# Another order of all operations, and each input tile laid out as its own block in memory, in an induced-attention and mixture-of-experts kernel

## Chip, cores and metric

One core of a Trainium2 chip, all arithmetic in fp32. The metric is the device time of one execution in microseconds (us). Before the change the median of three executions is 218.88 us (218.73 to 219.15).

## What is computed

Four batches of 11,456 points of 128 numbers pass through two attentions. In the first, 32 learned points attend to all points of a batch; in the second, every point attends to the 32 results. A mixture of eight experts with four slots each follows: softmax over all 45,824 points gives each slot its input, the experts work on 32 slot rows, and softmax over the 32 slots mixes their outputs back to every point.

```python
def mab(q, kv):
    s = scale * (q @ kv.transpose(0, 2, 1))
    s = s - s.max(-1, keepdims=True)
    a = np.exp(s)
    a /= a.sum(-1, keepdims=True) + 1e-09
    return a @ kv
h = mab(I, x)            # I: 32 learned points
x = mab(x, h)            # 45,824 rows of 128
logits = x @ phi         # 32 slots
d = softmax(logits, over all rows);  slot_input = d.T @ x
slot_out[e] = relu(slot_input[e] @ w1[e]) @ w2[e]     # e = 0..7
c = softmax(logits, over the 32 slots)
out = c @ slot_out
```

## The kernel before

The points are cut into 24 tiles, six to a batch (tiles 0 to 5 are batch 0, 6 to 11 batch 1, and so on), each of 15 blocks of 128 rows, 128 x 1920 numbers or 960 KB. A tile comes in twice, by rows (`xn`) and transposed (`xt`); for tiles 0 to 5 the transposed form is made on TensorE (`tp`, L294) and not loaded. All loads and stores are issued on SyncE's queue (SP), in the order of the program: loads of `xn` at L272, of `xt` at L282, of the expert weights `w` at L727, stores of the output at L989. Most large tiles share 13 buffers (the ring 'x'), for `xn`, `xt`, `w` and the output alike, so a load can start only when an earlier tile's last reader is done; `xt` of tiles 9 and 15, and of 10 and 16, each share a region inside the large tile `l_all`.

What each tile passes through, with the names used below (the number behind a name is the tile, or the batch for `u`, `ha`, `hp`, `hs`, `htp`, `hts`, `hb`, `gp`):

- **First attention.** `s1p` = scores on TensorE (L317), maximum on VectorE (`s1`, L328), maximum over a group of three tiles (`pm`, L356), exponential on ScalarE (L374), transpose on VectorE (`e1`, L377), sum over the points on TensorE (`ha`, L393). A batch ends with `hp`, `hs`, `htp` and `hts` (L441 to L455), which give the 32 results transposed, and `hb` (L467).
- **Second attention.** `s2p` = scores (L317, same helper), transpose on VectorE (`bt`, L563), maximum (`bm`, L566), subtraction on GpSimd (L570), exponential on ScalarE, transposes on TensorE (`tt`, L579), logits on TensorE (`lp`, L592), reciprocal of the sum (`bz`, L604), logits into `l_all` (L611), the scaled weights on GpSimd (L622).
- **Softmax over points.** Per segment of three tiles: `pt`, `mc`, `pb` give a running maximum; `d` on GpSimd or VectorE (L693), exponential, and `u` on TensorE (L706), which sums weighted rows per slot.
- **Softmax over slots.** Maximum `cm` (L498), `ct` = subtraction on GpSimd (L504, L507), exponential, sum `cz` (L528, or half sums `ch` on GpSimd at L519 for the tiles in the list CHALF), reciprocal (L534), product on GpSimd (L942), transpose on VectorE into `l_all` (L945).
- **Experts.** After the last `u`, slot inputs (`sit`), first layer `hpm` (L849), transposed hidden rows `htm` (L862), copied to `ma` and `mb` (L867), second layer `so` (L878). Beside it GpSimd forms `vs` and `vr` (L807 to L814), which `zpp` (L833) sums into the denominators `rz_l`; `sos`, `sr` and `srs` (L885 to L891) give the scaled result.
- **Output.** `po` on TensorE (L970) after `srs`, four PSUM tiles for one tile of points, evicted to `ot` by ScalarE or VectorE (L981; the lists OD and OD2 say which of the four VectorE takes), and stored in one to four pieces.

Nothing of the order is decided at run time or by a scheduler: about 1,090 operations are registered by name with their readers and writers, and the string ORDER, two base-62 digits to an operation, is the order in which their instructions are written. Each engine runs its own in that order.

Of the kernel before, what the change touches and what calls it, by code (L numbers as in the profile page):

```python
# [1099 lines left out]
```

## Time and profile before

| | |
|---|---|
| median of three executions | 218.88 us |
| the profiled execution | 219.14 us, its span 217.4 us |
| TensorE, VectorE, ScalarE, GpSimd busy | 86%, 75%, 63%, 58% |
| HBM read, written | 49.84 MB, 23.59 MB |
| first output matmul starts | 154.70 us |
| mean granted clock of TensorE | 0.919 |

Times in rows are microseconds from the start of the span. A row of a timeline gives start, duration and the instruction; in brackets stands the idle time of the engine before it and what ended it ("issue": nothing that the profile shows). PE is TensorE, PEld its weight loads, DVE VectorE, ACT ScalarE, POOL GpSimd. The 1.74 us by which the execution's own time exceeds the span lie around it.

### The profile page before, as it was taken

The numbers are of one execution on the slowest core, as the hardware profiler recorded it, in microseconds if no ns is written. First come the engines' busy times: TensorE is split into PE (matmuls) and PEld (weight loads), VectorE is DVE, ScalarE is ACT, GpSimd is POOL, SyncE is SP. The second block draws the span as 40 slices with busy tenths as digits, with TensorE's granted clock in tenths as the row PEclk, the third lists the DMA queues.
The fourth block names the chain that finished last, engine by engine and source line by source line (L and its number), as shares of the span: only waits on it lengthen the run. The fifth ranks groups of instructions, "written<-read, shape, count | busy, mean of one in ns | idle before, by whom it ended". The sixth has DMA issues, their size and how long they took to land.

```text
span 217.4 us, 6883 instructions
## 1 busy us (share of the span) xinstructions
PE 186.5 (86%) x2788; PEld 126.3 (58%) x2788; DVE 162.8 (75%) x374; ACT 136.0 (63%) x369; POOL 125.2 (58%) x138
## 2 busy tenths in 40 slices
PE   7699989999997999999999899998899988736400
PEld 7459565598543897539886399797546433212100
DVE  0114585999997999999998899967889878875400
ACT  3569441984653995358966688633599977963410
POOL 0000000557899798585998689999866855643000
PEclk9999999999999999999999999999996967975555
DMA  7999999998799999999999960000099999999994
GB/s 221 389 428 420 413 421 414 370 404 358 214 362 425 414 416 414 414 380 413 414 417 413 420 270 3 6 5 3 19 385 415 407 424 411 423 409 425 411 419 202
DMA packets 12414, 73.87 MB, mean 340 GB/s; under 512 B 1632, under 2 KB 2272, under 8 KB 12384
## 3 DMA queue, kind: packets, MB, share of 16 engines
q1 hardware_dynamic: 11952, 73.27, 83.6%
q8 instruction: 22, 0.36, 0.7%
q10 hardware_dynamic: 432, 0.17, 0.3%
q14 instruction: 8, 0.07, 0.1%
HBM read 49.84 MB, written 23.59 MB: 338 GB/s over the span
## 4 chain that ended last, share of the span: by engine, by line
PE 35%; DMA 28%; ACT 12%; DVE 9%; POOL 5%; issue 4%; SPq 1%; ACTq 0%; DVEq 0%; POOLq 0%
DMA xt<-xt 13%; ACT ot L981 8%; DMA out<-ot 8%; PE ha L393 7%; PE s2p L317 6%; PE lp L592 5%; DMA xn<-xn 4%; PE s1p L317 3%; PE tp L294 3%; DMA l_all<-xt 3%; PE tt L579 3%; PE so L878 2%; PE u L706 2%; POOL d L693 2%; PE po L970 1%
## 5 line engine op out<-in xcount | busy, mean ns | idle before, releaser
L970 PE MATMUL po<-l_all,srs 32*128 32x480 f32 x192 | 40.4, 780 | 9.7 <-DVE l_all L945 6.7
L981 ACT COPY ot<-po 128x480 f32<-128x480 f32 x65 | 33.0, 592 | 10.5 <-PE po L970 7.6
L970 PEld LDWEIGHTS po<-l_all,srs 32*128 32x128 f32 x192 | 17.6, 233 | 31.1 <-ACT ot L981 9.3
L570 POOL TENSOR_TENSOR bt<-bt,bm 128x480 f32<-128x480 f32 x24 | 23.6, 997 | 14.9 <-DVE bm L566 14.8
L942 POOL TENSOR_TENSOR ct<-ct,cz 128x480 f32<-128x480 f32 x24 | 23.8, 997 | 13.2 <-DVE cz L534 12.9
L592 PE MATMUL lp<-bdg,a2t 128*128 128x132 f32 x192 | 25.0, 277 | 0.4 <-issue 0.4
L328 DVE TENSOR_SCALAR_CACHE_REDUCE s<-s1p 128x480 f32<-128x480 f32 (+1 forms) x24 | 15.1, 643 | 13.5 <-PE s1p L317 13.0
L622 POOL TENSOR_TENSOR bt<-bt,bz 128x480 f32<-128x480 f32 x24 | 23.6, 1002 | 2.5 <-DVE bz L604 1.3
L507 POOL TENSOR_TENSOR ct<-l_all,cm 128x512 f32<-128x512 f32 x20 | 21.0, 1054 | 5.8 <-DVE l_all L945 4.0
L693 POOL TENSOR_TENSOR d<-l_all,m_all 128x512 f32<-128x512 f32 x19 | 21.8, 1169 | 4.0 <-ACT m_all L672 4.0
L592 PEld LDWEIGHTS lp<-bdg,a2t 128*128 128x128 f32 x192 | 23.1, 190 | 1.2 <-issue 1.1
L317 PE MATMUL s1p<-xt,it_sb 128*32 128x480 f32 x160 | 19.7, 571 | 2.9 <-DVE bm L566 1.6
L981 DVE COPY ot<-po 128x480 f32<-128x480 f32 x31 | 18.8, 635 | 3.7 <-PE po L970 3.7
L317 PE MATMUL s2p<-xt,hts 128*32 128x480 f32 x160 | 20.1, 570 | 0.6 <-issue 0.6
L374 ACT ACTIVATE s<-s,negm 128x480 f32<-128x480 f32 (+1 forms) x24 | 16.7, 701 | 4.9 <-DVE negm L359 4.9
L393 PE MATMUL ha<-xn,e 128*32 128x128 f32 x570 | 19.3, 274 | 0.0
L945 DVE STREAM_TRANSPOSE l_all<-ct 128x480 f32<-128x480 f32 x24 | 15.8, 662 | 4.4 <-POOL ct L942 4.1
L330 POOL MEMSET s<- 128x16 f32 x4 | 0.4, 111 | 31.0 <-DVE e L377 30.7
L511 ACT ACTIVATE ct<-ct 128x480 f32<-128x480 f32 x24 | 14.7, 621 | 5.7 <-POOL ct L507 5.6
L696 ACT ACTIVATE d<-d 128x512 f32<-128x512 f32 x24 | 14.9, 628 | 5.4 <-POOL d L693 4.2
L393 PEld LDWEIGHTS ha<-xn,e 128*32 128x32 f32 x570 | 16.5, 110 | 2.4 <-issue 0.9
L377 DVE STREAM_TRANSPOSE e<-s 128x480 f32<-128x480 f32 x24 | 15.5, 653 | 2.8 <-ACT s L374 2.4
(133 smaller groups left out, 372.1 us busy)
## 6 DMA issues: line engine op xcount, KB each, us to landing
out<-ot SPq DMA_DIRECT2D x20, 960.0 KB, 8.1
xn<-xn SPq DMA_DIRECT2D x18, 960.0 KB, 12.1
xt<-xt SPq DMA_DIRECT2D x14, 960.0 KB, 14.0
w<-w SPq DMA_DIRECT2D x8, 960.0 KB, 10.8
l_all<-xn SPq DMA_DIRECT2D x5, 960.0 KB, 9.5
l_all<-xt SPq DMA_DIRECT2D x4, 960.0 KB, 7.3
out<-ot SPq DMA_DIRECT2D x6, 480.0 KB, 4.9
out<-ot SPq DMA_DIRECT2D x4, 240.0 KB, 2.4
```

What stands on the lines that cost most here:

```text
L317: nc.tensor.matmul(dst[32 * g : 32 * g + 32, :w], lhs, src, start=True, stop=True)
L374: nc.scalar.activation(t[:, :v], t[:, :v], AF.Exp, bias=T["negm", b, g], accum_out=z6[:, a : a + 1])
L393: nc.tensor.matmul(ha[32 * q : 32 * q + 32, :P], T["e1", a][:, j * S : (j + 1) * S], T["xn", a][:, j * P : (j + 1) * P], start=c == lo and ...
L507: nc.gpsimd.tensor_tensor(t.rearrange("p (a e s) -> p a e s", s=S, e=2), l_blocks(n), m, op=ALU.subtract)
L570: nc.gpsimd.tensor_tensor(t, t, T["bm", n][:, :nb].unsqueeze(2).broadcast_to(full), op=ALU.subtract)
L592: nc.tensor.matmul(pt[:, q * 4 * SZ : (q * 4 + m) * SZ], t[: m * S, q * P : (q + 1) * P], bdgs[b % 2].rearrange("p q s -> p (q s)")[: m * ...
L622: nc.gpsimd.tensor_tensor(t, t, T["bz", n][:, :nb].unsqueeze(2).broadcast_to(full), op=ALU.mult)
L693: e.tensor_tensor(t.rearrange(o, s=S, e=2), l_pairs(n), m, op=ALU.subtract)
L942: nc.gpsimd.tensor_tensor(t, t, T["cz", n][:, :nb].unsqueeze(2).broadcast_to([P, nb, S]), op=ALU.mult)
L945: nc.vector.transpose(l_of(n), T[ck][:, :w])
L970: nc.tensor.matmul(ptile("mm", ("po", 4 * n + g))[:, :w], T["srs",][q, :], l_of(n)[q, :], start=True, stop=True)
L981: (nc.vector.tensor_copy if dve else nc.scalar.copy)(ot[:, g * w : (g + 1) * w], T["po", m][:, :w])
```

## The change

Three edits go together. First, a new ORDER string. Second, four lists: GpSimd's half sums are made for tile 22 and no longer for tile 10, and VectorE evicts 30 of the output's 96 pieces where it took 31. Third, the tensors in HBM: before, `xn` holds a batch as 128 long rows (46,080 bytes each) and `w` as 128 rows of 65,536 bytes, from which a tile's 7,680 bytes per row are cut; now each tile of `xn`, `xt` and `w` is one contiguous block of its own (H is 1, so `parts` changes nothing on the chip's side). The sizes of the transfers, the order of the loads and the layout of the output are as before.

```diff
@@ -34,36 +35,41 @@
...
-CHALF = [9, 10, 11, 12, 14, 16]
+CHALF = [9, 11, 12, 14, 16, 22]
...
-OD = [0, 1, 2, 7, 11, 15, 17, 18, 22, 23]
-OD2 = [0, 2, 3, 4, 5, 7, 8, 9, 10, 11, 12, 13, 14, 16, 17, 18, 19, 20, 21, 22, 23]
+OD = [0, 1, 2, 7, 11, 12, 15, 17, 18, 22, 23]
+OD2 = [0, 2, 3, 4, 7, 8, 9, 10, 11, 12, 13, 14, 16, 17, 18, 19, 21, 22, 23]
...
+H = 1
...
 ORDER = (
-    "000102030e0p0A0L0W3z3D0406080507090a0b0c0f0h0j0l0g0i0k0m0q0u0s0n0w0r0t0v0x0B0H0y0C0D0E0F0G0M0Q0d0o0z1718191a0O0S0N0I1f0
...
+    "000102030e0p0A0L0W0406080507090a0b0c0f0h0j0l0g0i0k0m0q0s0u0w0n0r0t0v0x0B0y0D0H0F0d0o0z17180M190C0E0G0I0N1a1f1i1g1j0Q0O0
...
 )
...
+SHAPES = {
+    "x0": (P, XW), "xn": (NT - 1, H, P, XW // H), "xt": (len(HOST_T), H, C, XW // H), "ind_t": (C, S), "phi": (C, S),
+    "w12": (NW, H, P, XW // H), "w3": (P, 2 * E * F - NW * WP), "consts": (P, 2 * P + 5),
+}
...
@@ -180,6 +186,9 @@
         o = l_end(tag) - XW
         T[kind, a] = l_all[:, o : o + XW]
         return T[kind, a]
+
+    def parts(t):
+        return t.rearrange("p (h w) -> p h w", h=H)
 
     def blocks(t):
         return t.rearrange("p (j s) -> p j s", s=S)
@@ -268,8 +277,10 @@
         def ldn(lo, hi):
             def f():
                 t = T["xn", a] if ("xn", a) in T else xtile("xn", a)
-                o = STARTS[c] * P
-                nc.sync.dma_start(t[:, lo:hi], xn[b, :, o + lo : o + hi])
+                if a:
+                    nc.sync.dma_start(parts(t), xn[a - 1].rearrange("h p w -> p h w"))
+                else:
+                    nc.sync.dma_start(t[:, lo:hi], x0[:, lo:hi])
 
             return f
 
@@ -279,7 +290,7 @@
         if a in HOST_T:
 
             def ldt():
-                nc.sync.dma_start(xtile("xt", a)[:, :xw], xt_d[HOST_T.index(a)][:, :xw])
+                nc.sync.dma_start(parts(xtile("xt", a)), xt_d[HOST_T.index(a)].rearrange("h p w -> p h w"))
 
             op("DMA", 2.50 * nb / 16, ("ldt", a), ldt, (), [("xt", a)], [(tag_of("xt", a), ("xt", a))])
             return
@@ -724,7 +735,10 @@
 
             def ld(o=o, m=m):
                 t = btile("x", ("w", o // WP))
-                nc.sync.dma_start(t[:, :m], w12[:, o : o + m])
+                if m == WP:
+                    nc.sync.dma_start(parts(t), w12[o // WP].rearrange("h p w -> p h w"))
+                else:
+                    nc.sync.dma_start(t[:, :m], w3)
                 wt.append(t)
 
             op("DMA", 2.50 * m / 2048, ("ldw", o // WP), ld, (), [("w", o // WP)], [("x", ("w", o // WP))])
@@ -1047,7 +1061,7 @@
...
-    xn = np.zeros((B, P, J * C), np.float32)
+    xn = np.zeros((NT, P, XW), np.float32)
...
@@ -1057,22 +1071,28 @@
...
-        xn[b, :, j0 * C : (j0 + nb) * C] = t.reshape(P, nb * C)
+        xn[a] = t.reshape(P, nb * C)
...
+    def cut(t):
+        return np.ascontiguousarray(t.reshape(-1, P, H, XW // H).transpose(0, 2, 1, 3))
+
...
+    w12 = np.concatenate([w1.reshape(C, E * F), w2.reshape(P, E * F)], axis=1)
...
-        "xn": xn,
-        "xt": xt,
+        "x0": xn[0],
+        "xn": cut(xn[1:]),
+        "xt": cut(xt),
...
-        "w12": np.concatenate([w1.reshape(C, E * F), w2.reshape(P, E * F)], axis=1),
+        "w12": cut(w12[:, : NW * WP].reshape(P, NW, WP).transpose(1, 0, 2)),
+        "w3": np.ascontiguousarray(w12[:, NW * WP :]),
...
```

Line numbers of the changed kernel are 9 to 14 higher. In the rows that follow, a name is followed by the tile (or batch) and then by a running number of the buffer.

**TensorE, end of batch 0's first attention.** Before:

```order
L317 MATMUL s1p_9_410<-l_all_78,it_sb_76 32x480 x4
L393 MATMUL ha_0_1_420<-l_all_78,e1_3_380 32x128 x15
L393 MATMUL ha_0_1_420<-l_all_78,e1_4_415 32x128 x15
L441 MATMUL hp_0_459<-zt_0_418,cst_70 128x1
L393 MATMUL ha_0_1_420<-l_all_78,e1_5_438 32x128 x15
L317 MATMUL s1p_10_476<-l_all_78,it_sb_76 32x480 x4
L317 MATMUL s1p_11_481<-xt_11_332,it_sb_76 32x480 x4
L452 MATMUL htp_0_501<-cst_70,hs_0_499 128x128
L467 MATMUL hb_0_505<-hs_0_499,cst_70 128x128
L317 MATMUL s2p_0_507<-xt_0_118,hts_0_503 32x480 x4
```

Now:

```order
L328 MATMUL s1p_8_394<-xt_8_334,it_sb_76 32x480 x4
L404 MATMUL ha_0_1_412<-l_all_78,e1_3_403 32x128 x15
L404 MATMUL ha_0_1_412<-l_all_78,e1_4_405 32x128 x15
L452 MATMUL hp_0_448<-zt_0_446,cst_70 128x1
L404 MATMUL ha_0_1_412<-l_all_78,e1_5_450 32x128 x15
L328 MATMUL s1p_9_467<-l_all_78,it_sb_76 32x480 x4
L328 MATMUL s1p_10_472<-l_all_78,it_sb_76 32x480 x4
L463 MATMUL htp_0_487<-cst_70,hs_0_485 128x128
L328 MATMUL s1p_11_493<-xt_11_338,it_sb_76 32x480 x4
L328 MATMUL s2p_0_509<-xt_0_114,hts_0_489 32x480 x4
```

The scores of tile 9 (`s1p_9`) stood in front of the sums `ha` of tiles 3 to 5 and stand behind them; `s1p_11` stood in front of `htp_0` and stands behind it; `hb_0` stood in front of the first `s2p` and stands further down.

**TensorE, scores of batch 2 among work of batches 0 and 1.** Before:

```order
L317 MATMUL s1p_14_1007<-xt_14_923,it_sb_76 32x480 x4
L317 MATMUL s1p_17_1016<-xt_17_927,it_sb_76 32x480 x4
L317 MATMUL s1p_15_1021<-l_all_78,it_sb_76 32x480 x4
L579 MATMUL tt_6_1038<-cst_70,bt_6_883 128x128 x3
L579 MATMUL tt_6_1038<-cst_70,bt_6_883 96x128
L579 MATMUL tt_7_1043<-cst_70,bt_7_889 128x128 x3
L579 MATMUL tt_7_1043<-cst_70,bt_7_889 96x128
L662 MATMUL pt_1_1048<-cst_70,tm_1_887 32x128 x3
L706 MATMUL u_0_950<-d_2_1030,bt_2_554 32x32 x15
L317 MATMUL s1p_16_1069<-l_all_78,it_sb_76 32x480 x4
```

Now:

```order
L328 MATMUL s1p_14_1005<-xt_14_898,it_sb_76 32x480 x4
L328 MATMUL s1p_16_1010<-l_all_78,it_sb_76 32x480 x4
L717 MATMUL u_0_970<-d_2_934,bt_2_604 32x32 x15
L328 MATMUL s1p_15_1039<-l_all_78,it_sb_76 32x480 x4
L673 MATMUL pt_1_1044<-cst_70,tm_1_845 32x128 x3
L590 MATMUL tt_6_1065<-cst_70,bt_6_847 128x128 x3
L590 MATMUL tt_6_1065<-cst_70,bt_6_847 96x128
L328 MATMUL s1p_17_1074<-xt_17_902,it_sb_76 32x480 x4
```

`s1p_17`, the sixth `xt` tile of its batch to be loaded, was the fourth of the six scores and is the last; `s1p_16`, `u` and `pt_1` moved ahead of it. In the same way `s1p_23` stood ahead of `s1p_22` and stands behind it. Some rows earlier, `s2p_10` was third of its group, behind `s2p_6` and `pt_0`; it is second now, ahead of both.

**GpSimd, experts.** Before:

```order
L748 MEMSET ma_2410 128x1440
L942 TENSOR_TENSOR ct_6_1408<-ct_6_1408,cz_6_1890 128x480
L507 TENSOR_TENSOR ct_8_2552<-l_all_78,cm_8_1647 128x512
L507 TENSOR_TENSOR ct_9_2554<-l_all_78,cm_9_1680 128x512
L942 TENSOR_TENSOR ct_7_1900<-ct_7_1900,cz_7_2157 128x480
L811 TENSOR_TENSOR vs_2559<-vs_2559,wl_2405 128x32
L519 TENSOR_TENSOR ch_9_2645<-ct_9_2554 128x240
L807 TENSOR_TENSOR vs_2559<-vs_2559,us_all_82 128x32
L814 TENSOR_TENSOR vr_2648<-vs_2559,us_all_82 128x128
L507 TENSOR_TENSOR ct_10_2652<-l_all_78,cm_10_1857 128x512
```

Now:

```order
L762 MEMSET ma_2468 128x1440
L825 TENSOR_TENSOR vs_2470<-vs_2470,wl_2405 128x32
L821 TENSOR_TENSOR vs_2470<-vs_2470,us_all_82 128x32
L956 TENSOR_TENSOR ct_5_1424<-ct_5_1424,cz_5_1661 128x480
L956 TENSOR_TENSOR ct_6_1426<-ct_6_1426,cz_6_1917 128x480
L956 TENSOR_TENSOR ct_7_1850<-ct_7_1850,cz_7_1921 128x480
L518 TENSOR_TENSOR ct_8_2552<-l_all_78,cm_8_1665 128x512
L828 TENSOR_TENSOR vr_2554<-vs_2470,us_all_82 128x128
L518 TENSOR_TENSOR ct_9_2580<-l_all_78,cm_9_1669 128x512
```

The product for `ct_5` was made much earlier and stands here now, and the two subtractions and the half sum in front of `vr` have become one subtraction. On TensorE `zpp`, which reads `vr`, stood behind `so` and stands between the two `htm`, in front of `so`; on VectorE one sum over slots (`cz_7`, L528), which stood behind batch 3's transposes, stands in front of them. Of the four pieces of the first output tile ScalarE evicts the first piece first, where it took the last first.

## Rows read from the trace of the kernel before

**Rows 1.** The windows view: busy time of each engine, clock, DMA share, GB/s, by stage.

```profile
37.10:54.00 16.90, 16.90 (x285) 13.04 (x288) 16.77 (x34) 11.94 (x36) 9.58 (x10) 1.00 0.97 386
54.00:57.00 3.00, 3.00 (x33) 0.89 (x32) 3.00 (x9) 2.87 (x9) 2.21 (x3) 1.00 0.32 90
57.00:125.00 68.00, 64.81 (x1229) 45.59 (x1225) 63.36 (x145) 45.09 (x137) 56.45 (x59) 1.00 1.01 405
125.00:153.70 28.70, 27.45 (x659) 24.82 (x655) 24.84 (x62) 17.47 (x55) 27.72 (x33) 1.00 0.14 54
163.00:207.00 44.00, 32.30 (x144) 13.66 (x143) 32.66 (x65) 32.20 (x74) 21.86 (x23) 0.72 1.02 416
```

**Rows 2.** TensorE's timeline, end of batch 0: start, duration, operation, idle before it.

```profile
28.79 1.01 PE L317 MATMUL s1p<-l_all,it_sb 128*32 128x480 f32 x8 [0.18 <-DMA l_all<-xt]
32.67 0.96 PE L393 MATMUL ha<-l_all,e 128*32 128x128 f32 x26 [0.49 <-issue]
35.60 0.39 PE L467 MATMUL hb<-hs,cst 128*128 128x128 f32 x2
36.05 1.01 PE L317 MATMUL s2p<-xt,hts 128*32 128x480 f32 x8
```

**Rows 3.** VectorE's timeline, first transpose of the second attention; a gap in batch 2.

```profile
37.13 0.68 DVE L563 STREAM_TRANSPOSE bt<-s2p 128x480 f32<-128x480 f32 x1 [0.62 <-PE s2p L317]
...
68.81 0.66 DVE L328 TENSOR_SCALAR_CACHE_REDUCE s<-s1p 128x480 f32<-128x480 f32 x1 [0.76 <-PE s1p L317]
```

**Rows 4.** TensorE's timeline, scores of batch 2.

```profile
64.31 1.02 PE L317 MATMUL s1p<-xt,it_sb 128*32 128x480 f32 x8
66.94 1.01 PE L317 MATMUL s1p<-xt,it_sb 128*32 128x480 f32 x8 [1.62 <-DVE bm L566]
68.69 1.09 PE L579 MATMUL tt<-cst,bt 128*128 128x128 f32 x8
```

**Rows 5.** The chain that ended last: the two transfers on it in mid-program.

```profile
57.02 9.79 DMA xt<-xt
66.87 18.69 DMA xt<-xt
```

**Rows 6.** TensorE's timeline, scores of batch 3.

```profile
95.85 1.82 PE L317 MATMUL s1p<-xt,it_sb 128*32 128x480 f32 x16 [0.44 <-ACT bt L573]
```

**Rows 7.** TensorE's timeline, the experts' second matmul.

```profile
149.01 1.95 PE L878 MATMUL so<-w,ma 128*32 128x128 f32 x64 [0.60 <-DVE ma L867]
```

**Rows 8.** GpSimd's timeline, batch 3 and experts.

```profile
129.00 1.95 POOL L622 TENSOR_TENSOR bt<-bt,bz 128x480 f32<-128x480 f32 x2 [0.65 <-DVE bz L604]
...
143.30 1.00 POOL L942 TENSOR_TENSOR ct<-ct,cz 128x480 f32<-128x480 f32 x1
148.56 0.45 POOL L814 TENSOR_TENSOR vr<-vs,us_all 128x128 f32<-128x128 f32 x1
148.97 1.06 POOL L507 TENSOR_TENSOR ct<-l_all,cm 128x512 f32<-128x512 f32 x1
```

**Rows 9.** ScalarE's timeline, first eviction.

```profile
155.93 2.41 ACT L981 COPY ot<-po 128x480 f32<-128x480 f32 x5 [0.71 <-PE po L970]
```

**Rows 10.** The chain that ended last: two pieces in which TensorE waited for its instructions.

```profile
114.38 0.41 issue
120.41 0.57 issue
```

**Rows 11.** VectorE's timeline, one sum over slots.

```profile
146.24 0.59 DVE L528 TENSOR_REDUCE cz<-ct 128x15 f32<-128x480 f32 x1
```

**Rows 12.** The windows view: a stretch of xn loads, one of w loads.

```profile
67.00:79.00 12.00, 12.00 (x189) 9.43 (x191) 10.45 (x29) 9.43 (x30) 9.98 (x12) 1.00 1.02 419
109.00:124.00 15.00, 14.02 (x336) 9.73 (x337) 13.05 (x28) 9.02 (x28) 12.49 (x13) 1.00 1.02 416
```

**Rows 13.** The page's part 6: the whole-tile stores.

```profile
out<-ot SPq DMA_DIRECT2D x20, 960.0 KB, 8.1
```

**Rows 14.** The page's part 5: the output matmuls and what they waited for.

```profile
L970 PE MATMUL po<-l_all,srs 32*128 32x480 f32 x192 | 40.4, 780 | 9.7 <-DVE l_all L945 6.7
```

More of the change, by code (lines that the diff above doesn't have):

```diff
@@ L27 @@
 WP = XW
+NW = 2 * E * F // WP
 FAR = -1.0e30
@@ L54 @@
-    "1U2i264j1V381W2j2H2I27282V2b4k291X2W2kcq2l484b4d2m4g2J2a2ncrcs1L2K4e4h4lcycGczcH392p2L4m2M4nctcucA2N2X2q2r2OcIcvcBcJ2P2Y3a5l4t5y4G2s3b2ZcC4o2t3c3d4p4r303ecw2o1Y4ucO2R4H4v4I312u2x4w"
-    "cx322y332v3f4q4T3g353h4J4K4s4x6i6m6q6u6y6d6h6l6p6t6x8T8X6f2w2z6j5L4U5m3j4VcD5z6g5n5A6n6k6o6z6r6s3i2Q2A2BcE4W5ocP4y4L3k3l2C6v4z4M5p2DcQ3m3n5q4A5M4X6w6A5N5BcK5CcW6BcL4B4C6CcRd44Y4N3o"
-    "5O3p3rcM3u344Z5r4O5P3q6D6E6F504P4D4Q51526GcFcN5D5Q5scS5E5F3s6I5t5R4E5G6L3t6J6H6K535ucTdc4ScX55cUd54F6U6O5S9195995H6M5v6P5I6R4R3v5T545J5w6N6Q8U6S6X5U6T6V568Y6Y576W928V6Z5XcV5xdd588Z"
@@ L63 @@
-    "gdgsgvgegfeygugmeJeGeKgwgngtgqgogpgrgxgWeHeLeReSeMeZhfhjhigLgPeThhf0feeNeOf1gOgNgXh0f2gYhgf3gZh3gMeUh1h7h6h4ePf4f5hlfmfuh5hneVf7f8eWhxhkh2hohmhph8hqgQhyhAhBh9hbhdf9fahahzeXfbhchrht"
-    "huhshvhefffgfhfnfcfdfvfofpfqfwhDhHfifrhGhEfsftfjhFhIhwfxhPhQfyfzfkflhShJhRhMfAhLfBhWhZhYi0hKhNhXhThUhChVi1hO"
-)
+    "000102030e0p0A0L0W0406080507090a0b0c0f0h0j0l0g0i0k0m0q0s0u0w0n0r0t0v0x0B0y0D0H0F0d0o0z17180M190C0E0G0I0N1a1f1i1g1j0Q0O0S0X130Z110P0Y0R0T1012141l1h1k0J3z3D3H3L3P3T3y3C0U150K0V161b1c"
+    "3E3A1d1m1n3I1e1o1r1p1s1u1x1y1q1t3B1z1B1C1v1w3M3Q1D3F3J1A1E1F1G1H3U3N3R3V3W3X1M1Z3Y1N3Z4043201O2141441I2S2E2c42451P22494c4f1Q46361R1K2d2e1J2F4i2G2T372U3847233G3K3O3S6e2f2H4a242g2h1S"
@@ new lines @@
+    "251T2I1U2i264j1V1W2V272W284k291X2J2j2k2acqcrcs2K484d4b4e2l394g4hcy2mct2n2L4l4m2pcz2b1Y2o2M4ncu2X1L2NcG4ocA2O2PcBcHcC2YcI5l5y2q4tcv2r2R4u4T2scwcO4vcJ4G4HcD4U2t3a3bcK3c2Z4p3d6i6m6q6u"
+    "6y6d6h6l6p6t6x6f5L4I4V2u2x2A4J4W2Q4wcL8T8X912y302v3e31344q323fcx334X6g3g6j352w2z5m6k6n6v2B2C4K3h3j4x2DcPcM6r3k5n5z3l5A6o6s6w5o5BcE4ycQ4z6z6A6B5M3m4L4A4Y3n5p5C4M4Z3o3r3p4BcN6C5q4N5N"
+    "cW4C5O5D6D3q6E5r3s4O6F5s4r50cR4D6I6G4P6J5P6LcS514s5t5E6H6K3t5QcFd46O52cT534Q6M6P3u3i4FcXcU4ScV5u4Edc5v5F5R5S5G4R6U6R6X546N6Q6S6Y8U6T5wcY3v5T565H6V575IcZ5U586Z8Y6W3w59705V719255d5dd"
@@ new lines @@
+    "8V8Z5W5a5J5Y3x72d05b5e5h7879937a7b735c807ld195999d8S8W9094989c7y7m7z968d5d9a9ed65i5f7c5g5j7n7A977o819b9f827B7C7p747d5Z7q7D757e7r7f7E9g609h617s9i83847F8e8f8g5K5x7g626366698hd7dkds9j"
+    "dA7h7t7u9k9l7i858i7G9n869o648q9m9p7H8r7v7I9q8j8s9r9t7j7J7w9u65878k769w9z67888ld85k7L9C9s9v9x8m899A9D7M9E8n7Nd27K5Xd38t8p7xde6a8udl7k8cdJ8a9y9B8v7O8o9F9G8w9Hdm8b9Ii2i38xdf7Qdn8y7P8z"
+    "8A687R8B9N6ba1af9O9PaH7T7W7U7X7S7VaV7Yb9a2aga3ahaIaWaJba8C9Q9Ra4a59J9S9KaXbbaibAbBbCbDbEbFbGbHbIaKbKaja69T77doakaYbc8D9Ua7aL7Z9Va8aMalaZa99Wd99X8EamaN9Yan8F8Gbd8Haaabb0acaO9Zadbeao"
@@ new lines @@
+    "a0apb1aPaqaeb28I8L8OaQbf8JdgasaRbLaSb38MataTbMbgaub4aUbhav8K9L8N8P8Qawbib5bjaxaAb6bkbN8Ray6c9Mb8bmi4i5i6i7i8bnazbOaraDbobQbRbPi9iabpbraBaEaCaFbqbUbSbubxblbVaGbsbWbvb7bYbybtbXibbZbw"
+    "bzdhc1bJbTc0c2c3dpicidc9cacbccc4c5dadidqdbdtc6cdcedjdRdre0cfc7cgchdudvc8e9cidBdCdKdDdEcjckclcmdwdxehdFdGeqdydHdzdScndLdMdNdTieifcocpigihfIdOdIeyfCfJfMfKdPfLdQdUe1fFdVfEeafDe2fGgEfR"
+    "gIebgHfVdWe3gGe4ecfUdXfTgFede5fSg4ggg7g8g5dYghgigkgjgyeee6eHe7dZePeXg6e8eieffXgBejerekeggAezgCgzesfYeletemgsgwgteueAgugXeneveweBfZeogZf5fdeCepg0g1gvh0h1gYgRgUgTgLgSgPeIeJgMexeQeDh3"
@@ new lines @@
+    "gNh6eKeLh7eEeMgOeFeGeYh4flgVeReSh5fNfPfQfOfHgKgJfWg9glgDgxh2g2g3gQgagdgbgegWh9eNeZgcgfh8f0haf1eOgmgphcf2f6gqeTf7f8eUf3f4fuhfhbhjhdf9hignhgeVeWfegohhfahxhBffgrhzhyhAhehChrhufgfbfmfc"
+    "fhfifjfvhvhDhsfnhthlhHhEhFhGfkhJfofphofqfrfsfthnhKhmhMhphNhPhRhwhkhIhQhLhOhUhqhShTfwfxfyfzfAfBhWhYhZi0hXi1hV"
+)
+SHAPES = {
+    "x0": (P, XW), "xn": (NT - 1, H, P, XW // H), "xt": (len(HOST_T), H, C, XW // H), "ind_t": (C, S), "phi": (C, S),
+    "w12": (NW, H, P, XW // H), "w3": (P, 2 * E * F - NW * WP), "consts": (P, 2 * P + 5),
+}
@@ L141, in tile_kernel @@
 @with_exitstack
-def tile_kernel(ctx, tc, xn, xt_d, ind_t, phi, w12, consts, out):
+def tile_kernel(ctx, tc, x0, xn, xt_d, ind_t, phi, w12, w3, consts, out):
     nc = tc.nc
```

8 lines of the change are left out of this document (removed).

## Prediction

> **What bounds the kernel now.** I read the windows view first. Between the first transpose of the second attention (37.13) and the end of the experts (153.70), TensorE is busy 16.90 + 3.00 + 64.81 + 27.45 = 112.16 of 116.6 us [rows 1], so it has 4.4 us of gaps, spread over all of the middle. VectorE has 8.6 us by the same rows. This change leaves the amount of work as it is, so up to the first output matmul it can only close gaps or open others. After that the transfers bound: from 163 to 207 the DMA share is 1.02 at 416 GB/s, while TensorE, VectorE and ScalarE are busy 32 of 44 us [rows 1]; 23.59 MB at 416 GB/s are 56.7 us, whatever the order. So a time saved ahead of the first store counts in full, if the store queue never runs dry.
>
> Second, the timelines of TensorE and VectorE, where the gaps stand with what ended them. On TensorE I find one of 1.62 us at 66.94 [rows 4], 0.49 at 32.67 and 0.18 at 28.79 [rows 2], 0.44 at 95.85 [rows 6] and 0.60 at 149.01 [rows 7]. Third, the chain that ended last. It holds two pieces, 0.41 and 0.57, in which TensorE waited for nothing visible [rows 10]; I take these, and the 0.49, for the arrival of the next block of its instructions. The chain also runs through the transfers of two `xt` tiles, 57.02 to 66.81 and 66.87 to 85.56 [rows 5].
>
> **Batch 0's end.** TensorE's work in front of the first `s2p` is the same but for `hb_0`, whose successor starts 0.45 us after it (35.60 to 36.05) [rows 2] and which goes behind. The 0.18 that `s1p_9` waited for its transfer is covered now, since `ha` of tiles 3 to 5 stands in front. `s1p_11` moves from in front of `htp_0` to behind it, where it fills the time in which ScalarE makes `hts`, but the path from `htp_0` to `s2p_0` then holds a whole `s1p`, so this gains nothing by itself. VectorE still has to finish `s1_11` before its first transpose, which waited 0.62 us for `s2p` [rows 3]. Bounds: nothing, and 0.45 + 0.18 + 0.49 = 1.1 if the block of instructions comes in time too. I take -0.3, nearer the end at which that gap stays, for nothing moved makes instructions come sooner.
>
> **Batch 2.** `s1p_17` waits 1.62 us on TensorE, and its wait is put down to a `bm` [rows 4]; yet its tile landed at 66.81 [rows 5], 0.13 us before it started, so I put it down to the transfer. VectorE then idles 0.76 for the scores [rows 3]. Now two more `s1p` (0.87 us each, as 66.94 to 68.69 is two of them), `tt_6` (half of 1.09), `pt_1` and a `u` stand between [rows 4]: over 2.1 us, so the landing is covered even if it comes no earlier. It should come earlier: the DMA share is 0.32 from 54 to 57 [rows 1], a hole of 2.0 us in which `xt` 15 to 17 wait for their places, and `s2p_10`, which frees one, now runs ahead of `s2p_6`, about 1 us sooner. Bounds: nothing and -1.62. I take -1.3, near the full gap, since the rows that cover it need nothing that lands later.
>
> **Batch 3.** `s1p_23` ahead of `s1p_22` cost 0.44 [rows 6]; in the order of the loads most of it goes: bounds 0 and -0.44, taken -0.3. Against it, `cz_7`, 0.59 us [rows 11], now stands in front of batch 3's transposes on VectorE, and behind it wait the transposes, `bm`, and from there GpSimd: it waits 0.65 for a `bz` at 129.00 [rows 8] and is then nearly without a gap to the experts (27.72 of 28.7 busy from 125) [rows 1]. Bounds 0 and +0.59; I take +0.4, since a late VectorE is late 1:1 here, and some rows of that batch move the other way.
>
> **Experts.** `so` waited 0.60 for the copy `ma` [rows 7], which stood behind other work on VectorE. Now `zpp` stands in front of it and needs `vr`. On GpSimd, between the end of the memset, where the first product starts (143.30), and `vr` there are now two `vs` (an estimate of 0.3 each, from the 0.45 of the larger `vr`), three products at 1.00 and a subtraction at 1.06 [rows 8], 4.7 us: `vr` starts at about 148.0, not 148.56, and ends at 148.4. `zpp` and the second `htm` follow, so `so` starts at about 148.8. Bounds -0.60 (no wait left) and +0.65 (GpSimd late once more by its longest wait in rows 8); I take -0.2.
>
> **First store.** ScalarE waited 0.71 for the last of four pieces [rows 9] and now begins with the first. The bounds are 0 and -0.71. I take -0.2, because all four pieces are needed soon after.
>
> **Blocks of instructions.** TensorE's stream is as long and its gaps of 0.41 to 0.57 [rows 2, 10] are cut at other places. I take one more on the path, +0.5; bounds -1.5 (the three shown fall beside other work) and +1.5 (three more do not).
>
> **Layout and lists.** The windows of `xn` (rows of 46,080 bytes before) and of `w` (65,536) moved 419 and 416 GB/s at a share of 1.02 [rows 12], while the kernel's output, which keeps its layout, goes at the same 416 [rows 1]. So I cost contiguous tiles at nothing. [...] One eviction and one half sum change engine in stages with over 10 us to spare on ScalarE: nothing.
>
> **The sum.** -0.3 - 1.3 - 0.3 + 0.4 - 0.2 - 0.2 + 0.5 = -1.4 us, on the profiled execution's 219.14, or 217.7. That execution lies 0.26 above the median of 218.88, so I predict **217.5**.
>
> **Rivals.** A measurement of this kernel tells about 0.2%, 0.44 us, from no change.
>
> (a) *The gain is taken back by the loads.* From 57 to 125 the DMA share is 1.01 [rows 1], and the chain goes from `xt_17` straight to `xt_19`, 18.69 us [rows 5]. If the loads do not start earlier, the gap that closes at 66.94 opens again at the scores of tile 19, after 85.56, and the -1.3 and -0.3 of batches 2 and 3 are lost: +0.2 in all, 219.1. For it: no slack in the transfers for 68 us. Against: the 2.0 us hole in front, which the earlier `s2p_10` closes by about half. Chance 0.15.
>
> (b) *Slower: the output's queue runs dry.* `po` waited 6.7 us in all for VectorE's transposes [rows 14], and this costs nothing today because a store lands a median of 8.1 us after issue [rows 13] where 0.98 MB at 416 GB/s take 2.4: some 5.7 us of other stores lie ahead of it. Stores are issued in the order of the program on one queue, and that order is new (tiles 9, 8, 13, 11 and 12 come early now). If a transpose or a sum for an early tile comes later than the queue is long, each us counts in full; this decides from about 6 us of lateness on, or less in the first 10 us, when the queue is still short. With 3 us dry, half of the 6.7: 220.5. For it: the first tiles' softmax is what was moved most. Against: 26% to spare on all engines there. Chance 0.12.
>
> (c) *Full closing.* All gaps named go and no block is late: -1.1 - 1.6 - 0.4 - 0.6 - 0.2, that is -3.9, or 215.0. Chance 0.12.
>
> (d) *The blocks of instructions come later throughout*, because the transfers are denser: three more gaps on the path, +1.5 - 0.5 on the sum: 218.5, no change. Chance 0.06.
>
> **How the numbers follow.** The forecast, -1.4 with its bounds, has 0.55: 216.4 to 218.4, nearly all of it faster. With (c), and half of what its upper end leaves, faster is 0.66; no change 0.15, from the middles of (a) and (d); slower 0.19, from (b) and the upper parts of (a). The range takes in (a) and (d) with half a microsecond above them, and reaches close to (c), leaving out (b): 215.3 to 219.6.
>
> **What would show it.** Right: in the changed profile the gap in front of `s1p_17` is under 0.3 us and that of `s1p_23` gone; the share of DMA between 54 and 57 is above 0.6; the first transpose of the second attention starts at about 36.8, `so` at about 147.3, the first eviction about 1.5 us before 155.93; the DMA share stays at 1.0 from there to the end. Wrong: the first store is early but the end is not (b), the gap stands again after `xt_19`'s landing (a), or packets of `w` are faster than before.

## The result, and the profile after

| | before | changed |
|---|---|---|
| median of six executions each | 218.57 us (217.90 to 219.15) | 220.97 us (219.83 to 221.59) |
| profiled execution, its span | 219.14, 217.4 us | 221.34, 219.3 us |
| busy: TensorE, VectorE, ScalarE, GpSimd | 86%, 75%, 63%, 58% | 87%, 75%, 63%, 57% |

The ratio is 1.0107, 95% interval 1.0072 to 1.0141: slower by about 1%, where 217.5 us and a gain were forecast.

The windows view of the changed kernel, cut as in [rows 1] (busy time of TensorE, its weight loads, VectorE, ScalarE, GpSimd; granted clock; DMA share; GB/s):

```profile
37.10:54.00 16.90, 16.90 (x286) 13.04 (x282) 16.41 (x34) 12.41 (x38) 9.25 (x10) 1.00 0.97 388
54.00:57.00 3.00, 3.00 (x29) 0.78 (x27) 3.00 (x9) 1.86 (x8) 3.00 (x4) 1.00 0.36 79
57.00:125.00 68.00, 64.72 (x1192) 46.86 (x1188) 62.50 (x143) 43.98 (x133) 52.65 (x55) 0.97 0.98 399
163.00:207.00 44.00, 36.11 (x152) 18.54 (x150) 33.03 (x67) 34.68 (x79) 25.12 (x26) 0.79 1.01 416
```

TensorE's gaps from 57 to 125 are as large as before (3.3 us against 3.2 in [rows 1]), so what was closed was paid again in the same stretch; and the clock, 1.00 before, is 0.97. Both have their place in TensorE's timeline. Its gaps for instructions ("issue" as the releaser) are these three:

```profile
32.30 0.74 PE L404 MATMUL ha<-l_all,e 128*32 128x128 f32 x18 [0.85 <-issue]
...
67.70 0.56 PE L328 MATMUL s1p<-l_all,it_sb 128*32 128x480 f32 x1 [1.43 <-issue]
...
116.16 0.31 PE L590 MATMUL tt<-cst,bt 128*96 128x128 f32 x1 [1.33 <-issue]
```

Together 3.61 us, against 0.49 + 0.41 + 0.57 = 1.47 before [rows 2, 10]. The gaps that the change was to close are gone: `s1p_17` no longer waits 1.62 [rows 4], `s1p_23` no longer 0.44 [rows 6]:

```profile
70.52 1.01 PE L328 MATMUL s1p<-xt,it_sb 128*32 128x480 f32 x8
...
96.55 1.82 PE L328 MATMUL s1p<-xt,it_sb 128*32 128x480 f32 x16
```

Behind the third gap the granted clock falls (windows of 1 us):

```profile
115.00:116.00 1.00, 0.00 (x0) 0.00 (x0) 1.00 (x3) 0.00 (x0) 1.00 (x2) 1.00 1.02 422
...
117.00:118.00 1.00, 1.00 (x7) 1.00 (x7) 0.53 (x1) 0.88 (x5) 0.57 (x1) 0.52 1.05 423
118.00:119.00 1.00, 1.00 (x6) 1.00 (x6) 0.65 (x1) 0.37 (x3) 0.00 (x0) 0.50 1.03 422
119.00:120.00 1.00, 1.00 (x17) 0.82 (x19) 0.00 (x0) 0.06 (x1) 0.00 (x0) 0.50 1.02 422
120.00:121.00 1.00, 1.00 (x38) 0.60 (x38) 0.65 (x2) 0.82 (x3) 0.36 (x1) 0.78 1.02 422
```

TensorE did nothing from 114.8 to 116.2, and from 117 to past 120 its granted clock was 0.50 to 0.52. By the four rows from 117 on that took away 0.48 + 0.50 + 0.50 + 0.22 = 1.7 us of TensorE's full speed (an estimate). VectorE idled 1.55 us there in front of a `bz` at 120.24; batch 3's first transpose came at 121.41, where it came at 117.96 before.

The following marks are the starts of the first instruction of each kind in the timelines of the profiled executions (us).

| kernel | first `bt` | `bt` tile 17 | `bt` tile 18 | memset `ma` | `so` | `srs` | first store | end of span |
|---|---|---|---|---|---|---|---|---|
| before | 37.13 | 106.17 | 117.96 | 142.04 | 149.01 | 153.65 | 156.51 | 217.4 |
| changed | 37.20 | 106.58 | 121.41 | 143.91 | 150.69 | 156.02 | 158.76 | 219.3 |

Up to tile 17 the two are within 0.4 us of each other; between tiles 17 and 18 the changed kernel loses 3.0 us, as much as the gap of 1.33 and the 1.7 at half clock together; from there to the memset it takes 1.6 less than the kernel before, so that 1.5 are lost from tile 17 to the memset. From the memset to `srs` it loses 0.5; from the first store to the end it is 0.3 faster.

### The profile page after: what moved, and what is told of

It is laid out like the page before. It is cut to its first block, busy times and chain, and to the rows that moved or that the text cites. A ratio compares the mean times of both kernels' runs of the same rounds, so it can differ in the third digit from the quotient of the medians.

```text
span 219.3 us, 6890 instructions
## 1 busy us (share of the span) xinstructions
PE 191.3 (87%) x2788; PEld 131.7 (60%) x2788; DVE 163.6 (75%) x373; ACT 137.6 (63%) x370; POOL 125.3 (57%) x138
## 5 line engine op out<-in xcount | busy, mean ns | idle before, releaser
L984 PE MATMUL po<-l_all,srs 32*128 32x480 f32 x192 | 43.3, 724 | 8.6 <-DVE l_all L959 6.1
L995 ACT COPY ot<-po 128x480 f32<-128x480 f32 x66 | 33.5, 594 | 11.2 <-PE po L984 11.2
L984 PEld LDWEIGHTS po<-l_all,srs 32*128 32x128 f32 x192 | 21.4, 215 | 29.1 <-ACT ot L995 9.0
L603 PE MATMUL lp<-bdg,a2t 128*128 128x132 f32 x192 | 26.0, 283 | 0.0
L603 PEld LDWEIGHTS lp<-bdg,a2t 128*128 128x128 f32 x192 | 24.1, 196 | 0.3 <-ACT a2t L597 0.2
L328 PE MATMUL s2p<-xt,hts 128*32 128x480 f32 x160 | 19.1, 572 | 0.0
L584 ACT ACTIVATE bt<-bt 128x480 f32<-128x480 f32 x24 | 14.3, 604 | 5.6 <-POOL bt L581 5.6
L404 PEld LDWEIGHTS ha<-xn,e 128*32 128x32 f32 x570 | 16.0, 109 | 2.8 <-issue 1.0
```

What stands on the lines that cost most here:

```text
L328: nc.tensor.matmul(dst[32 * g : 32 * g + 32, :w], lhs, src, start=True, stop=True)
L404: nc.tensor.matmul(ha[32 * q : 32 * q + 32, :P], T["e1", a][:, j * S : (j + 1) * S], T["xn", a][:, j * P : (j + 1) * P], start=c == lo and ...
L603: nc.tensor.matmul(pt[:, q * 4 * SZ : (q * 4 + m) * SZ], t[: m * S, q * P : (q + 1) * P], bdgs[b % 2].rearrange("p q s -> p (q s)")[: m * ...
L984: nc.tensor.matmul(ptile("mm", ("po", 4 * n + g))[:, :w], T["srs",][q, :], l_of(n)[q, :], start=True, stop=True)
L995: (nc.vector.tensor_copy if dve else nc.scalar.copy)(ot[:, g * w : (g + 1) * w], T["po", m][:, :w])
```

## Experiments

Theory A, formed on these rows: the new order runs into late blocks of TensorE's instructions, and the clock with them. Rivals: the layout (L), the experts with `zpp` in front (Z), TensorE's instruction density alone (D). Each kernel was timed beside the kernel before, to which the ratios refer; one, marked as such, was timed a single time. A profile shows one execution: those of order alone, of `lp` moved and of `zpp` moved took 219.49, 219.84 and 219.24 us, among the quickest of their kernels (medians 220.33, 220.78, 220.60), so their gaps may be shorter than the usual ones.

**Layout alone and order alone.** The two halves of the change apart.

```diff
 # layout alone: the changed kernel with
-ORDER, CHALF, OD, OD2 of the changed kernel
+ORDER, CHALF, OD, OD2 of the kernel before
 # order alone: the kernel before with
-ORDER, CHALF, OD, OD2 of the kernel before
+ORDER, CHALF, OD, OD2 of the changed kernel
```

> The order and lists of before, with the inputs laid out as contiguous tiles. Theory A (the loss is made by the new order, through TensorE's instruction blocks: in the changed kernel's trace it stands still 1.33 us at 114.8 for its instructions and then runs at the lower clock until 120.4): no change against before, within 0.4 us, gaps of TensorE for its instructions as before (0.4 to 0.6 us each). Rival L (contiguous tiles change the transfers, and so the time at which instruction blocks come): at least 1 us slower than before, with a gap of over 1 us on TensorE.

> The new order and lists, with the inputs laid out as before. Theory A: as slow as the changed kernel, 1.0 to 3.0 us over before, with a gap of over 1 us on TensorE near 115 and a stretch at half clock behind it. Rival L: as fast as before or faster (217 to 218.9), with no gap over 0.6 us.

Layout alone: ratio 1.0036 (1.0000 to 1.0072), gaps for instructions of 0.28 and 0.57. Order alone: 1.0070 (1.0040 to 1.0099). So the order does most of it, by these two values. The layout is not told apart from no change, nor from a third of the loss or more; its rate did not change (420 and 414 GB/s in the two windows of [rows 12]), and the gap of over 1 us that rival L asks for did not come. Order alone shows these gaps in TensorE's timeline beyond 100, and no fall of the clock (1.00 from 112 to 124):

```profile
114.56 0.32 PE L579 MATMUL tt<-cst,bt 128*96 128x128 f32 x1 [0.65 <-issue]
122.26 0.58 PE L706 MATMUL u<-d,bt 128*32 128x32 f32 x42 [1.09 <-issue]
```

The expected gap of over 1 us near 115 was 0.65, and the half clock did not come; a gap of 1.09 came one block later. The gap thus sits at the same instruction (the last `tt` of its tile) with another length.

**The dense stretch broken up.** In the changed kernel `lp` of tiles 15 and 16 goes between two pairs of `ha` (and two `bz` of ScalarE behind two of its other rows).

```diff
 TensorE:
-lp 15, lp 16, hb, ha 20, ha 21, hp, pt, ha 22, ha 23
+hb, ha 20, ha 21, lp 15, lp 16, hp, pt, ha 22, ha 23
```

> The changed kernel with one edit: the logits lp of tiles 15 and 16 stand between the sums ha of tiles 21 and 22, instead of in front of those of tile 20, so that 256 instructions of TensorE last longer just in front of the gap at 114.8. Theory A: the gap shrinks from 1.33 to under 0.5 us and the half clock behind it goes; VectorE's transposes of batch 3 come 2 to 3.5 us earlier, and the whole is 1.0 to 2.0 us faster than the changed kernel (219.0 to 220.0). Rival Z (the loss is made in the experts, where zpp stands in front of so and waits for GpSimd): within 0.5 us of the changed kernel.

Ratio to before 1.0104 (1.0048 to 1.0161), against 1.0107 of the changed kernel: nothing gained. TensorE's timeline beyond 100:

```profile
108.35 1.95 PE L404 MATMUL ha<-xn,e 128*32 128x128 f32 x60 [1.09 <-DVE e L388]
...
122.61 0.58 PE L717 MATMUL u<-d,bt 128*32 128x32 f32 x42 [1.09 <-issue]
```

The gap near 115 is gone, as expected, the clock stays whole (1.00 from 104 to 124), and batch 3's first transpose comes at 118.73 instead of 121.41. But `ha`, now earlier, waits 1.09 for VectorE, and the next block comes 1.09 late. The time of the kernel did not follow: in this execution a gap taken out at one place stands at two others.

**`zpp` behind `so` again,** in the changed kernel.

```diff
 TensorE:
-htm, zpp, htm, so
+htm, htm, so, zpp
```

> The changed kernel with one edit: zpp and its reciprocal stand behind so again, as before the change. Theory A: 0.3 to 0.6 us faster than the changed kernel at most, since so waited about that long for zpp, and the gap near 115 stays. Rival Z: 1.5 to 2.5 us faster, back at the time of before.

Ratio 1.0102 (1.0069 to 1.0135). Rival Z falls. `so` came 6.53 us after the memset (6.78 with `zpp` in front, 6.97 before), yet `srs` came no sooner. The gap near 115 was there, and so was the half clock, in a second trace:

```profile
113.83 0.32 PE L590 MATMUL tt<-cst,bt 128*96 128x128 f32 x1 [1.06 <-issue]
```

The windows view of the same kernel, just behind that gap:

```profile
115.00:116.00 1.00, 1.00 (x8) 0.91 (x7) 0.55 (x2) 0.98 (x4) 0.51 (x1) 0.71 1.11 446
116.00:117.00 1.00, 1.00 (x6) 0.92 (x5) 0.31 (x1) 0.00 (x0) 0.00 (x0) 0.50 0.95 392
117.00:118.00 1.00, 1.00 (x35) 0.62 (x38) 0.39 (x2) 0.80 (x3) 0.10 (x1) 0.50 1.00 415
```

**Late weights.** The loads of the expert weights run from 95 to 125 and are not read before 143. Here they wait for batch 3's `hs`, by a one-column copy into the first of their tiles; the transfers then stand still while TensorE goes through the sums of batch 3.

```diff
+if o == 0:
+    nc.scalar.copy(t[:, :1], T["hs", B - 1][:, :1])
 nc.sync.dma_start(...)         # and the nine loads placed behind hs in ORDER
```

> The changed kernel, but the loads of the expert weights wait until batch 3's hs is made (about 115), so that the transfers stand still while TensorE goes through its densest instructions (105 to 115). Theory A (TensorE's instruction blocks come late because they queue behind the loads): the gaps at 114 and at 122, 0 to 1.33 us each in the four traces with the new order, fall under 0.2 us, the clock stays whole there, VectorE's last transpose of batch 2 to its first of batch 3 takes under 12.2 us (14.8 in the changed kernel, 11.8 before), and the kernel is 1.0 to 2.0 us faster than the changed one: ratio to before 1.000 to 1.006. Rival D (the gaps come from the density of TensorE's instructions alone, whatever the loads do): gaps and time as in the changed kernel, ratio 1.007 to 1.013.

> The changed kernel with late loads of the expert weights, a second time, beside the one before it. Theory A: a gap of about 1.1 us at 67, none over 0.3 us between 100 and 125, ratio to before 0.995 to 1.001.

> The kernel before the change, with the same late loads of the expert weights. Theory A: its two gaps of 0.41 and 0.57 near 115 and 121 go, and it is 0.5 to 1.0 us faster than before (ratio 0.995 to 0.998). Rival D: no change, or slower if the weights come too late.

> The kernel before with late loads of the expert weights, a second time, beside the next. Theory A: ratio to before 0.987 to 0.993 again.

| kernel | ratio to before, late weights | without |
|---|---|---|
| changed | 0.9978 (0.9948 to 1.0008); again 0.9992 (0.9952 to 1.0031) | 1.0107 |
| before | 0.9897 (0.9861 to 0.9934); again 0.9915 (0.9883 to 0.9947) | 1 |

Rival D falls: the instructions are as dense as before, and with idle transfers the gaps from 100 to 125 are gone in three of the four traces. In both traces of the kernel before, a gap of 0.53 or 0.54 stands at 132 to 134 instead, where the loads now run (share 1.03 and 1.00 from 126 to 134; 0.65 and 0.02 without the delay, and no gap). The windows of the changed order with late weights, first run, show a share of 0.13 and TensorE without a gap:

```profile
108.00:114.00 6.00, 6.00 (x140) 5.36 (x139) 5.96 (x14) 5.34 (x19) 5.87 (x7) 1.00 0.13 52
...
116.00:128.00 12.00, 12.00 (x248) 8.59 (x247) 11.70 (x23) 8.65 (x27) 11.73 (x13) 1.00 0.99 407
```

In its second run the gap near 115 is absent too, but one of 0.98 stands at 121.31, when the weights are on their way; the expected "none over 0.3" failed there. The gain is larger than expected for the kernel before (0.5 to 1.0 us expected, about 2 found; the two gaps that went are 1.0 of it, the rest was not placed) and for the changed one (1.0 to 2.0 expected, 2.5 to 2.8 found), and the kernel before with late weights is the best of all: 216.77 and 217.30 us median.

So the weights' loads cost both orders 2 to 3 us. How much of the change's loss is their doing, the times do not settle: with late weights the distance between the orders is 0.8% (0.9978 / 0.9897, and 0.9992 / 0.9915), against 1.07% without, and each ratio is known to 0.3 or 0.4%. The profiled executions say more of one stage, from tile 17's `bt` to the memset. It took 37.33 us in the changed kernel and 35.87 in the one before. With late weights it took 34.40 in the changed kernel's first run and 34.53 and 34.54 in the kernel before; the second run of the changed one, with its gap of 0.98, took 35.51. Without a late block this stage costs both orders the same, so the 1.5 us lost there in the profiled execution are the late block's doing and the clock's.

**The scores alone.** The kernel before with the prediction's largest term and nothing else.

```diff
 TensorE:
-s1p 14, s1p 17, s1p 15, ..., s1p 16;  s1p 21, s1p 23, s1p 22
+s1p 14, s1p 15, ..., s1p 16, s1p 17;  s1p 21, s1p 22, s1p 23
```

> The kernel before the change with one part of the change alone: the scores of tile 17 stand behind those of tile 16, and those of 23 behind 22. If the prediction's step on batches 2 and 3 was right by itself, the 1.62 us gap at 66.94 goes and the kernel is 1.0 to 1.6 us faster (ratio 0.993 to 0.996). Theory A in its strong form (a gap that closes is followed by a late instruction block): TensorE's gaps for instructions grow by half a microsecond or more, and the ratio is 0.997 to 1.001.

> The two before together, on the kernel before the change. Theory A: the gains add, 1.5 to 2.5 us faster than before (ratio 0.988 to 0.993). If either part gives nothing, the other alone.

Alone: 1.0007 (0.9973 to 1.0041), no change. With late weights 0.9927 (0.9891 to 0.9963), no better than late weights alone. The gap at 66.94 went, and this is where it is now:

```profile
83.48 1.01 PE L317 MATMUL s1p<-xt,it_sb 128*32 128x480 f32 x8 [1.64 <-DMA xt<-xt]
85.82 1.01 PE L317 MATMUL s1p<-xt,it_sb 128*32 128x480 f32 x8 [0.46 <-DMA xt<-xt]
```

2.10 us of waiting for batch 3's `xt`, where the trace of before has 0.16 in all:

```profile
85.69 1.01 PE L317 MATMUL s1p<-xt,it_sb 128*32 128x480 f32 x8 [0.16 <-DMA xt<-xt]
```

TensorE came to batch 3's scores earlier, and the transfers did not: the first two of their tiles landed at 83.34 and 85.68, against 83.21 and 85.56 before. This is rival (a) of the prediction, whole. The wait wanders between the two places by itself as well: in the six traces that keep the old order of the scores, the gap in front of `s1p_17` and the waits for `xt` at batch 3's scores together come to 1.3 to 2.5 us, and with the scores moved to 2.10 and (with late weights) 2.00. The expected growth of gaps for instructions did not show (0.26 and 0.53 are left).

**Sixteen more instructions at the start.** Timed once, to see whether the gaps belong to operations or to a count.

```diff
-warm_into(ptile("mm", ("warm0",)), 8)
+warm_into(ptile("mm", ("warm0",)), 12)
```

> The kernel before with four more matmuls in the row of dummies at the start (16 more instructions with their weight loads, in time in which TensorE waits for the first tile). Theory A (instructions come in blocks of a fixed number): the gaps for instructions, which before stand in front of the last 26 of a row of ha, the last 7 of a row of lp and the last 11 of a row of s2p, move 8 matmuls towards the start: 34 of ha left, then a few of the ha in front of that lp, then 19 of s2p or the row in front of it. Rival (a gap belongs to an operation): the gaps stay at 26, 7 and 11. The time: within 0.5 us of before.

The time of this single execution was 216.67 us, 2.4 under the median of before beside it, where it was expected within half a microsecond. Of the gaps, the first two are not there; the third is. TensorE's timeline of the kernel before, from the gap to the next `gp`:

```profile
120.98 1.41 PE L317 MATMUL s2p<-xt,hts 128*32 128x480 f32 x11 [0.57 <-issue]
121.83 0.55 PE L706 MATMUL u<-d,bt 128*32 128x32 f32 x5
122.22 0.57 PE L317 MATMUL s2p<-xt,hts 128*32 128x480 f32 x1
122.22 0.19 PE L706 MATMUL u<-d,bt 128*32 128x32 f32 x1
122.22 0.57 PE L317 MATMUL s2p<-xt,hts 128*32 128x480 f32 x1
122.25 0.79 PE L706 MATMUL u<-d,bt 128*32 128x32 f32 x24
```

The same stretch of TensorE's timeline with the sixteen instructions added:

```profile
118.68 0.23 PE L706 MATMUL u<-d,bt 128*32 128x32 f32 x3 [0.81 <-issue]
118.71 0.60 PE L317 MATMUL s2p<-xt,hts 128*32 128x480 f32 x2
118.74 0.20 PE L706 MATMUL u<-d,bt 128*32 128x32 f32 x2
118.77 1.78 PE L317 MATMUL s2p<-xt,hts 128*32 128x480 f32 x14
120.33 0.50 PE L706 MATMUL u<-d,bt 128*32 128x32 f32 x30
```

11 + 5 + 1 + 1 + 1 + 24 = 43 matmuls stood behind the gap, and 3 + 2 + 2 + 14 + 30 = 51 do now: eight more, which with their weight loads are the sixteen instructions added. The gap stands at a count of instructions, not at an operation.

All traces bear this out, when TensorE's instructions (matmuls, weight loads and its semaphore instructions) are counted from the start: each of the 34 gaps of over 0.2 us put down to "issue", in sixteen traces, has a multiple of 256 plus 193 or 194 of them in front of it (706, 3521 and 3777 in the kernel before, 705, 1729 and 3522 in the changed one). And each ends 2.25 to 2.65 us after a packet of 16 KB starts on the page's instruction queue q8; for the gap at 116.16 that packet starts at 113.56. So these gaps are waits for the next block of 256 instructions.

**The gap at 67.** In the changed kernel with late weights, batch 2's row tiles are held back as well, by the same kind of copy: until 60.4 in the first kernel, until 63 in the second, where the six loads also stand further down in ORDER.

```diff
 t = T["xn", a] if ("xn", a) in T else xtile("xn", a)
+if a == 12:
+    nc.scalar.copy(t[:, :1], T["hs", 1][:, :1])
```

> [...] Theory A: the gap of 1.15 us for instructions at 67.3 falls under 0.4 us, and the kernel is 0.4 to 1.0 us faster than with late weights alone (ratio to before 0.993 to 0.997), if the held-back loads don't make it wait at the scores of batch 3 instead. Rival E (the gap at 67 has nothing to do with the loads): gap of 1 us or more as before, ratio 0.996 to 1.000.

> The changed kernel with late loads of the expert weights, and with batch 2's row tiles held back further, until about 63, so that the transfers have really stood still before the block of instructions for 67 is due (held until 60.4 they never did). Theory A: a hole in the transfers between 62 and 65, the gap for instructions at 67 under 0.5 us (1.15 to 1.74 without the hole), and the time equal to or up to 1.0 us below late weights alone, since the hole costs the loads about as much as TensorE gains; a wait for xt at batch 3's scores of up to 1.5 us may open. Rival E (the gap at 67 does not depend on the loads): a gap over 1 us stays.

Held to 60.4: ratio 1.0022 (0.9988 to 1.0057), the gap 1.74 (1.15 without). The transfers were hardly idle from 57 to 66 (share 0.89 in the first microsecond, 0.96 to 1.07 in the others), so this told little of the theory, and the expectation that the gap would shrink was wrong. Held to 63: 0.9970 (0.9935 to 1.0004), the gap 0.34, and the share 0.86 from 62 to 64 and 0.90 from 64 to 66. Without the hold, on the same chip, the gap was 0.52. That is no proof: in the eight traces with the new order this gap reads 1.43, 0.25, 0.25, 0.25, 1.15, 0.52, 1.74 and 0.34, and in none of the old order is there one. It belongs to the new order: there the packet of this block starts at 63.3 to 65.9, in the eight traces with the old one at 56.3 to 59.7. What delays it, and how far the loads set the gap's length, stays open.

**Two pieces of the change on the best kernel.**

```diff
 # the kernel before with late weights
-ScalarE's evictions of tile 1: piece 3, 0;  stores: piece 3, 2, 0, 1;  VectorE: cm 14, ma
+ScalarE's evictions of tile 1: piece 0, 3;  stores: piece 0, 2, 3, 1;  VectorE: ma, cm 14
```

> The kernel before with late loads of the expert weights and two pieces taken from the change: ScalarE evicts the first piece of the first output tile first and its store goes first, and the copy ma stands one row earlier on VectorE. By the prediction's steps on the experts and the first store, 0.3 to 0.8 us faster than with late weights alone (ratio 0.985 to 0.990). If those steps were wrong, the same as late weights alone.

0.9942 (0.9915 to 0.9969): nothing gained over late weights alone, 0.9915 beside it. `so` came 6.39 us after the memset instead of 6.97 and the first store 14.35 instead of 14.47, but the stage from the first store to the end of the span took 61.3 us in that execution, against 60.7 and 60.5 in the two traces of late weights alone.

## Why the prediction was wrong

**Batch 2, -1.3: the step that failed.** "The landing is covered even if it comes no earlier" was right, and the gap in front of `s1p_17` went. What failed is that this was counted as a gain. Alone, it gave nothing (1.0007): the time was waited for again at the next transfers, 1.64 and 0.46 us. I had rival (a) with this mechanism, its place and 0.15; the rows for it (a share of 1.01 for 68 us, `xt_17` and `xt_19` back to back on the chain) weighed more than I let them. In the whole change the wait for `xt` does not come back. "It should come earlier" held there: `xt_17` landed at 64.51 instead of 66.81 and batch 3's first tiles at 82.26 and 84.60, 1.0 sooner, though the hole from 54 to 57 stayed (share 0.36; over 0.6 was to show it). There a gap for instructions of 1.43 stands instead, at 67.70, and from the first `bt` to tile 17's the changed kernel takes 69.4 us against 69.0. In the four traces of this order in which that gap is 0.34 or less, the same stretch takes 68.2 to 68.3, so some of the gain is there when the block is in time; the old order's traces spread from 67.9 to 69.9.

**Blocks of instructions, +0.5: the term that was mis-sized.** I took the "issue" gaps for blocks of instructions, which the count of 256 and the packets bear out. I allowed one more gap of half a microsecond, and bounded it by three. There are still three, but longer ones: they grew from 0.41 to 0.57 each to 0.85 to 1.43, from 1.47 to 3.61 in all, by 2.1 us, and behind one of them the clock fell, another 1.7, for which there was no term. Each gap was priced at half a microsecond, as those of before, as if a block could not come later than that. Rival (d) named this, priced its blocks at +1.5, which by my sum made no change, and had a chance of 0.06. How near this lay could have been read before: all three gaps of before stand where transfers fill the DMA engines (share 1.00 from 31 to 33, 1.01 from 57 to 125). That an order that closes other gaps brings the next block's first instruction forward, while the block itself comes no sooner, is argued and not shown.

That queue, the larger of the page's two for instructions, reads 22 packets and 0.36 MB in both kernels, or 16 KB to a packet; TensorE's 5674 and 5682 instructions, divided by 256, are 22.2. How far ahead a block is asked for, no run here shows.

**Batch 0, -0.3.** Nothing came of it: the first `bt` started at 37.20 instead of 37.13. The 0.18 for the transfer went, and the gap in front of `ha` grew from 0.49 to 0.85.

**Batch 3, -0.3 + 0.4.** The 0.44 went. VectorE's lateness can't be read apart from the 3.0 us lost between tiles 17 and 18 in this execution; with late weights, where no gap stands there, the new order takes 11.8 to 11.9 us from the one tile to the other and the old one 11.2.

**Experts, -0.2, and first store, -0.2.** `so` came 0.19 earlier after the memset (6.78 instead of 6.97), and the store 0.12 earlier after `srs` (2.74 instead of 2.86). But between `so` and `srs` 0.69 was lost, which no term held. VectorE's timeline of the changed kernel:

```profile
152.88 0.40 DVE L539 TENSOR_REDUCE cz<-ch 128x15 f32<-128x240 f32 x1 [0.66 <-POOL ch L530]
153.20 0.24 DVE L545 RECIPROCAL cz<-cz 128x15 f32<-128x15 f32 x1
153.35 0.63 DVE L509 TENSOR_REDUCE cm<-l_all 128x16 f32<-128x512 f32 x1
153.91 0.23 DVE L545 RECIPROCAL cz<-cz 128x15 f32<-128x15 f32 x1
154.06 0.62 DVE L509 TENSOR_REDUCE cm<-l_all 128x16 f32<-128x512 f32 x1
154.60 0.66 DVE L959 STREAM_TRANSPOSE l_all<-ct 128x480 f32<-128x480 f32 x1
155.19 0.25 DVE L899 COPY sos<-so 128x128 f32<-128x128 f32 x1
```

`so` was done at 154.4. `sos` waits behind a sum that GpSimd's `ch` makes late, two `cm` and a transpose. Before, the same sum stood at 149.07, and `sos` started as soon as `so` was done (149.01 and 3.70 us, 152.71):

```profile
149.07 0.39 DVE L528 TENSOR_REDUCE cz<-ch 128x15 f32<-128x240 f32 x1
...
152.78 0.29 DVE L885 COPY sos<-so 128x128 f32<-128x128 f32 x1
```

I had followed GpSimd's queue to `vr` and stopped there, and not asked what else waits for it. All eight traces with the new order take 14.8 to 15.0 us from the memset to the first store, those with the old one 14.3 to 14.5. That `sos` makes this difference is read from the trace; no run moved it alone.

**Output.** Right: the stage is set by the transfers (share 1.01 at 416 GB/s from 163 to 207), 60.5 us from the first store to the end of the span in the new order, 60.9 before. Rival (b), most of my case for slower, did not occur. **Layout at nothing** stands within its interval.

What the parts come to in the two profiled executions, whose spans differ by 1.9 us: 0.1 up to the first `bt` and 0.3 from there to tile 17, where the gaps at 32 and 67 stand; 1.5 from tile 17 to the memset, the late block and the clock; 0.4 from the memset to the first store (0.7 between `so` and `srs`, less 0.3 gained on either side); -0.3 after it. Over all executions less is settled. The later first store is some 0.2% and in every trace, the layout 0 to 0.7% by its interval, the weights' loads nothing to about 0.8%; with late weights 0.8% stay between the orders, and what makes them was not taken apart. The prediction's 0.2% for telling two kernels apart was also too small: the intervals here reach 0.3% and more to each side.

## What to carry to other kernels

Where TensorE is nearly full and the transfers too, a gap that an order closes is no gain until it is shown what TensorE reaches sooner: the next tile, or the next block of its own instructions, may be what it waits for then (here the 1.62 us closed at 66.94 became 2.10 at batch 3's scores). A wait for a block of instructions has no fixed price: here it was 0.25 to 1.74 us. Follow every engine past the operation that was moved, to the next one that some other engine waits for. Loads that were not needed for a while cost something here although they were hidden: moving the expert weights behind the densest stretch gained 0.9%, more than any reordering here.
